# First layer and gates of a channel mix from softmax weights and packed values times the weight matrix, as a two-tap filter with three products for two tokens

## The chip, the cores and the metric

The kernel runs on one core of one Trainium2 chip. The metric is the time of one execution on the device in microseconds (us). The engines are named as the profile names them: PE is TensorE's matmul, PEld its weight load, DVE is VectorE, ACT is ScalarE, POOL is GpSimd, SP is SyncE, whose queue issues all DMAs here.

## The reference

```python
def sm_attn(qq, kk, vv):                       # softmax(scale * qq kk^T) vv
    ...
p_packed = sm_attn(p, k, v)                    # 32 packed rows for each head
out = sm_attn(q, p_packed, p_packed)           # 576 rows for each head
x = out.transpose(0, 2, 1, 3).reshape(B, S, H * D)
x_prev = np.concatenate([zeros, x[:, :-1, :]], axis=1)
xk = mu_k * x + (1.0 - mu_k) * x_prev
xr = mu_r * x + (1.0 - mu_r) * x_prev
k = np.maximum(xk @ w_k, 0.0)
v = k * k @ w_v
r = 1.0 / (1.0 + np.exp(-(xr @ w_r)))
return r * v
```

There are 8 sequences (B) of 576 tokens (S), 8 heads (H) of 64 columns (D), 32 packed rows for each head, 512 model columns and 1024 hidden columns. Weights come as 64-bit numbers and are turned into fp32 on the core. Everything is kept to fp32 accuracy: a product of two fp32 matrices is made of three products of a rounded part ("high", fp32r) and a rest ("low", fp32r): high by high, high by low, low by high.

## The kernel before, in words

The program is written as small generators, one for each piece of work. A planner (class Flow) holds a free time for each engine, costs such as `vec(n)` and `pe(us)`, pools of buffers with slots, and ranks; it takes the piece that could start first, ties by rank, and so fixes, at build time, the order of each engine's instructions. On the chip each engine then works through its list in that order.

For each sequence b, `front` makes the scores of the 32 packed rows of 8 heads (line 437, PE), `weights_of` their softmax, and the packed values `pm` (line 461, PE; 128 partitions are 4 head pairs by 32 rows, two heads side by side). They are transposed to `ppT` (line 482). `back` then does, for each half of the tokens, the scores of the tokens (line 541, PE), a softmax over 32 packed rows on transposed data (lines 553 to 576, mostly DVE, with one ACT exponential), and, at line 584 on PE, weights times packed values: that is x, with channels on partitions. `mixed_in` copies x from PSUM on ACT (line 606).

From there the work goes by 9 blocks of 512 tokens. `mix` makes xk and xr of a block on ACT and DVE (lines 639 and 643), `split` makes their high and low parts (lines 659 and 661). `gates` multiplies xr by w_r (lines 717 to 719, tile `pr`), `keys` multiplies w_k by xk (lines 678 to 680, tile `ph`), `values` multiplies the squared keys `sq` by w_v (lines 746 to 748, tile `pvo`). Each of these is a run of PE instructions of 512 columns. `squared` does relu, square, high part and low part (lines 689, 692, 696, 698); `gated` does the sigmoid (line 728); `done` multiplies (line 757) and writes 128 tokens by 512 columns to HBM with one DMA. `convert` loads a piece of a weight matrix and turns it into fp32 (lines 285 to 291) and into high and low parts (295, 297). In the first 50 us, while PE waits, the planner puts in matmuls without use (line 817, tile `spare`), so that PE's clock stays up.

PSUM has four slots `m` of one bank for the block matmuls and two slots `pa` of two banks for everything else.

Of the kernel before, what the change touches and what calls it, by code (L numbers as in the profile page):

```python
# [163 lines left out]
def attn_pack_channel_mix(ctx: ExitStack, tc: tile.TileContext, q, k, v, p, mu_k, mu_r, w_k, w_v, w_r, out):  # L164
# [5 lines left out]
    NG = H // 4  # L170
    NPR = H // 2
    HS = S // 2
    NTB = S // 32
    NQ = 4 * P
    NC = DM // P
    NF = DF // P
    TB = 512
    NB = B * S // TB
    NT = TB // P
    WP = 512  # L180
    scale = 1.0 / float(D) ** 0.5
    eps = 1e-9

    flow = Flow()


    FIRST = 10.09, 10.29
    RANK_1, RANK_MIX, RANK_W, RANK_V, LOADS_1 = 14.28, 11.5, 13.6, 15.2, 14.29
# [7 lines left out]
    def act(n, after=None, table=None):  # L196
        return "scalar", 0.14 + 0.72e-3 * n, after, table

    def pool(n, after=None):
        return "gpsimd", 0.1 + 2.2e-3 * n, after, None  # L200
# [14 lines left out]
    TR = dict(kT=0.0, qT=0.0)  # L215
    HALVES = slice(0, 64), slice(64, P)

    def reached():

        yield None, 0.0, None, None  # L220

    EARLY = 2
# [4 lines left out]
    BUFS = dict(raw=3, kq=4, vt=2, pt=1, a=2, aT=1, pm=2, e=2, a2=1, xt=4, tmp=4, xk=NC, sq=NF, sig=4,  # L227
                pa=2, both=1, m=4, staged=4)
# [9 lines left out]

    for tag in ("mx", "nmx", "rs", "sm", "free"):
        for j in range(2 if tag != "free" else 1):
            const.tile([P, 1 if "m" == tag[0] or "n" == tag[0] else 2], F32, name=f"{tag}{j}", tag=f"{tag}{j}")
    for tag, n, size in (
        ("xk", NC, 2 * TB), ("sq", NF, 2 * TB), ("tmp", 4, WP), ("sig", 4, DM), ("kq", 4, S), ("a", 2, S),
        ("raw", 3, S), ("a2", 1, S), ("e", 2, S), ("aT", 1, 5 * P), ("vt", 2, NPR * 4 * D),
    ):
        for j in range(n):
            sb.tile([P, size], F32, name=tag, tag=f"{tag}{j}")

# [5 lines left out]
    mus = const.tile([P, 4, NC], F32, name="mus")  # L256
# [3 lines left out]
    wk_h = const.tile([P, NC, DF], F32R, name="wk_h")  # L260
    wk_l = const.tile([P, NC, DF], F32R, name="wk_l")
    wr_h = const.tile([P, NC, DM], F32R, name="wr_h")
    wr_l = const.tile([P, NC, DM], F32R, name="wr_l")
    wv_h = const.tile([P, NF, DM], F32R, name="wv_h")
    wv_l = const.tile([P, NF, DM], F32R, name="wv_l")

    def convert(w, hi, lo, c, o, n, event, first=None):

        rank = flow.now.rank
        if first:  # L270
            flow.now.rank = first
        staged = yield from flow.take("staged")
        slot = yield from flow.take("sq")
        st = tile_([P, 2 * WP], U32, "sq", slot, "st")
        yield from load(st[:, :2 * n], w[c * P:(c + 1) * P, o:o + n].bitcast(U32), 0.46, 3.5e-3 * n)
        flow.now.rank = rank
        yield from reached()
        sm = yield from flow.take("tmp")
        m = tile_([P, WP], U32, "tmp", sm, "m")[:, :n]
        w0, w1 = (st[:, :2 * n].rearrange("p (n two) -> p two n", two=2)[:, j, :] for j in range(2))  # L280

# [8 lines left out]
        flow.give("sq", slot)  # L292
        flow.give("staged", staged)
        yield act(n)
        nc.scalar.copy(hi[:, c, o:o + n], m.bitcast(F32))
        yield vec(n)
        nc.vector.tensor_tensor(lo[:, c, o:o + n], m.bitcast(F32), hi[:, c, o:o + n].bitcast(F32), op=ALU.subtract)
        flow.give("tmp", sm)
        flow.set(event)

    ts, vts, pts, xts, xt2 = {}, {}, {}, {}, {}
# [8 lines left out]
    def loads(b):  # L310
        flow.spawn(packed(b), lrank(b) - (0.03 if b else 0.015))
        for src, tag in ((k, "kT"), (v, "vt"), (q, "qT")):
            if tag == "vt":
                for h in range(2):
                    flow.spawn(values_of(b, h), lrank(b) - 0.01)
                continue
# [529 lines left out]
```

## Time and profile before

| what | value |
|---|---|
| runs of before | 605.46, 605.8 (median), 606.75 us |
| profiled execution | span 605.1 us (first to last instruction) |
| mean granted TensorE clock | 0.997 |
| PE busy | 593.7 us, 98% of the span |
| DVE busy | 363.9 us, 60% |
| ACT busy | 331.0 us, 55% |
| DMA | 49.43 MB, mean 82 GB/s |

The profile's own execution is one whose span is 0.7 us below the median of the runs; the rest of the program's time lies around the span. In the rows of a timeline, the first number is the start in us from the start of the span, the second how long the row's group lasted, and "xN" how many instructions it holds. An fp32 matmul instruction appears as two records (the order of the program has 30 `spare` matmuls where the timeline has 60), an fp32r matmul and a transpose as one. A busy PE is not a PE at its peak: a matmul lasts longer than the step from its start to the start of the next.

### The profile page before, as it was taken

The numbers are of one execution on the slowest core, as the hardware profiler recorded it, in microseconds if no ns is written. First come the engines' busy times: TensorE is split into PE (matmuls) and PEld (weight loads), VectorE is DVE, ScalarE is ACT, GpSimd is POOL, SyncE is SP. The second block draws the span as 40 slices with busy tenths as digits, with TensorE's granted clock in tenths as the row PEclk, the third lists the DMA queues.
The fourth block names the chain that finished last, engine by engine and source line by source line (L and its number), as shares of the span: only waits on it lengthen the run. The fifth ranks groups of instructions, "written<-read, shape, count | busy, mean of one in ns | idle before, by whom it ended". The sixth has DMA issues, their size and how long they took to land.

```text
span 605.1 us, 10174 instructions
## 1 busy us (share of the span) xinstructions
PE 593.7 (98%) x3984; PEld 471.1 (78%) x3984; DVE 363.9 (60%) x701; ACT 331.0 (55%) x579; POOL 2.1 (0%) x23
## 2 busy tenths in 40 slices
PE   8899999999999999999999999999999999999997
PEld 7787777777777777777877787778788888888886
DVE  1499999949688479556765577166503822451321
ACT  4478784775774648454845485457534803641420
POOL 0000000000000000000000000000000000000000
PEclk9899999999999999999999999999999999999999
DMA  8895561764634646346034702000010010001001
GB/s 189 248 266 136 216 155 34 166 126 88 113 60 137 118 70 139 99 74 143 1 103 64 144 1 72 20 1 0 26 45 1 0 70 0 2 0 71 0 2 69
DMA packets 159184, 49.43 MB, mean 82 GB/s; under 512 B 143776, under 2 KB 151968, under 8 KB 159136
## 3 DMA queue, kind: packets, MB, share of 16 engines
q1 hardware_dynamic: 159136, 48.79, 34.0%
q8 instruction: 31, 0.51, 0.3%
q14 instruction: 17, 0.14, 0.1%
HBM read 39.33 MB, written 9.44 MB: 81 GB/s over the span
## 4 chain that ended last, share of the span: by engine, by line
PE 84%; DVE 5%; ACT 4%; SPq 3%; DMA 2%; issue 1%; ACTq 0%
PE pvo L746 11%; PE ph L678 10%; PE pvo L747 10%; PE pvo L748 10%; PE ph L680 10%; PE ph L679 10%; PE pr L717 5%; PE pr L719 5%; PE pr L718 5%; SPq L207 3%; PE pa L461 2%; PE pa L584 2%; DMA st<-in_moe_w_r 1%; PE pa L541 1%; ACT x L639 1%; DVE m L289 1%
## 5 line engine op out<-in xcount | busy, mean ns | idle before, releaser
L678 PE MATMUL ph<-xk,wk_h 128*128 128x512 f32 x288 | 114.8, 399 | 0.0
L746 PE MATMUL pvo<-wv_h,sq 128*128 128x512 f32 x288 | 113.9, 395 | 0.0
L679 PE MATMUL ph<-xk,wk_h 128*128 128x512 f32 x288 | 112.4, 390 | 0.0
L680 PE MATMUL ph<-xk,wk_l 128*128 128x512 f32 x288 | 112.3, 390 | 0.0
L747 PE MATMUL pvo<-wv_l,sq 128*128 128x512 f32 x288 | 112.3, 390 | 0.0
L748 PE MATMUL pvo<-wv_h,sq 128*128 128x512 f32 x288 | 112.2, 390 | 0.0
L689 ACT ACTIVATE r<-ph 128x512 f32<-128x512 f32 x72 | 43.0, 598 | 90.7 <-PE ph L680 89.7
L696 DVE CAST sq<-r 128x512 fp32r<-128x512 f32 x72 | 30.3, 420 | 100.6 <-ACT r L692 98.4
L746 PEld LDWEIGHTS pvo<-wv_h,sq 128*128 128x128 f32 x288 | 54.1, 188 | 15.9 <-issue 4.5
L678 PEld LDWEIGHTS ph<-xk,wk_h 128*128 128x128 f32 x288 | 54.1, 188 | 15.5 <-issue 4.5
L643 DVE SCALAR_TENSOR_TENSOR x<-xt,mus,x 128x512 f32<-128x512 f32 (+7 forms) x128 | 60.4, 513 | 6.0 <-ACT x L639 5.9
L680 PEld LDWEIGHTS ph<-xk,wk_l 128*128 128x128 f32 x288 | 54.1, 188 | 11.5
L748 PEld LDWEIGHTS pvo<-wv_h,sq 128*128 128x128 f32 x288 | 54.1, 188 | 11.4
L639 ACT ACTIVATE x<-xt,mus 128x512 f32<-128x512 f32 (+7 forms) x128 | 62.0, 530 | 1.5 <-DVE xr L661 1.3
L747 PEld LDWEIGHTS pvo<-wv_l,sq 128*128 128x128 f32 x288 | 54.1, 188 | 10.7
L679 PEld LDWEIGHTS ph<-xk,wk_h 128*128 128x128 f32 x288 | 54.2, 188 | 10.3
L717 PE MATMUL pr<-wr_h,xr 128*128 128x512 f32 x144 | 58.7, 408 | 0.0
L719 PE MATMUL pr<-wr_h,xr 128*128 128x512 f32 x144 | 56.7, 394 | 1.0 <-DVE xr L661 1.0
L718 PE MATMUL pr<-wr_l,xr 128*128 128x512 f32 x144 | 56.3, 391 | 0.0
L728 ACT ACTIVATE sig<-pr 128x512 f32<-128x512 f32 x36 | 21.3, 601 | 60.1 <-PE pr L719 56.5
L698 DVE TENSOR_TENSOR sq<-r,sq 128x512 fp32r<-128x512 f32 x72 | 49.4, 686 | 1.4
L757 DVE TENSOR_TENSOR sig<-pvo,sig 128x512 f32<-128x512 f32 x36 | 23.9, 686 | 38.8 <-PE pvo L748 38.8
(80 smaller groups left out, 727.5 us busy)
## 6 DMA issues: line engine op xcount, KB each, us to landing
out<-sig SPq DMA_DIRECT2D x36, 256.0 KB, 2.1
vt<-in_v SPq DMA_DIRECT2D x16, 512.0 KB, 4.6
raw<-in_k SPq DMA_DIRECT2D x96, 72.0 KB, 2.8
raw<-in_q SPq DMA_DIRECT2D x96, 72.0 KB, 2.8
st<-in_moe_w_k SPq DMA_DIRECT2D x8, 512.0 KB, 6.0
st<-in_moe_w_v SPq DMA_DIRECT2D x8, 512.0 KB, 5.5
raw<-in_k SPq DMA_DIRECT2D x16, 144.0 KB, 2.9
raw<-in_q SPq DMA_DIRECT2D x16, 144.0 KB, 5.1
```

The lines of the kernel that those rows point to most:

```text
L639: nc.scalar.mul(x32[:, o:o + n], xts[b, c][:, 1 + s:1 + s + n], mus[:, j, c:c + 1])
L643: nc.vector.scalar_tensor_tensor(x32[:, o:o + n], xts[b, c][:, s:s + n], mus[:, j + 1, c:c + 1], x32[:, o:o + n], op0=ALU.mult, op1=ALU.add,)
L678: nc.tensor.matmul(ph, wk_h[:, c, fs], xh, start=(c == 0), stop=False)
L679: nc.tensor.matmul(ph, wk_h[:, c, fs], xl, start=False, stop=False)
L680: nc.tensor.matmul(ph, wk_l[:, c, fs], xh, start=False, stop=(c == NC - 1))
L698: nc.vector.tensor_tensor(hl[:, 1, :], r, hl[:, 0, :].bitcast(F32), op=ALU.subtract)
L717: nc.tensor.matmul(pr, xh[:, ts_], wr_h[:, c, :], start=(c == 0), stop=False)
L718: nc.tensor.matmul(pr, xh[:, ts_], wr_l[:, c, :], start=False, stop=False)
L719: nc.tensor.matmul(pr, xl[:, ts_], wr_h[:, c, :], start=False, stop=(c == NC - 1))
L746: nc.tensor.matmul(pv[t], sh, wv_h[:, f, :], start=(f == 0), stop=False)
L747: nc.tensor.matmul(pv[t], sh, wv_l[:, f, :], start=False, stop=False)
L748: nc.tensor.matmul(pv[t], sl, wv_h[:, f, :], start=False, stop=(f == NF - 1))
```

## The change

The packed values times the weight matrix are made once for each sequence, and the tokens' softmax weights A multiply that directly; x, xk and xr are no longer made. With G = packed values times w, and Gm = (mu times packed values) times w, a token's row of xk times w_k is A[t] Gm + A[t-1] (G - Gm). For a pair of tokens, even e and odd o, and the odd token before it, that is

- y0 = A[e] G, shared by the pair,
- even token: y0 + (A[o before] - A[e]) (G - Gm),
- odd token: y0 + (A[o] - A[e]) Gm.

These are three products for two tokens, each over 256 rows (8 heads by 32 packed rows, two PE passes of 128) where before each token's product ran over 512 channels (four passes). Tokens are ordered by even and odd (288 each), and all outputs have channels on partitions, so that each sequence is one unit of 576 tokens.

New or changed: `taps` multiplies the packed values (plain, times mu_k, times mu_r: tile `pps`) by a chunk of 256 columns of w_k or w_r in fp32 (line 683, 16 instructions a chunk, 6 chunks a sequence), `taps_of` makes from it G, Gm and G - Gm with high and low parts (tile `G`, three buffers); `prep` makes the three moving operands `ehl` (one buffer) with high and low parts from `even` and `odd`; `main` runs the three products (line 748, tile `y`, 288 columns) and then `values` (line 815, tile `pvo`, 288 columns); `summed` drains y: ACT copies y0 to both places' common half, DVE adds the other two (line 775); then relu, two squares and the low part, or the sigmoid. `done` multiplies, transposes 32 by 32 on DVE and writes 32 partitions at a time, 128 bytes a piece, with four DMAs for each 128 channels. For the first sequence (`WHOLE = 1`) taps and products are plain fp32 without high and low parts. w_k and w_r are only turned into fp32; w_v still gets high and low parts. Buffers: raw 3 to 2, vt 2 to 1.

```diff
-        ppT = sb.tile([P, P], F32, name="ppT", tag="ppT")
+        pp = tile_([P, 3, P], F32, "pps", s3)
...
+        for j in range(2):
+            yield vec(P)
+            nc.vector.tensor_tensor(pp[:, 1 + j, :] ..., pp[:, 0, :] ..., mus[:, j, :] ..., op=ALU.mult)
...   # back(): up to the softmax over 32 rows as before, then
-        nc.vector.transpose(a2.rearrange("p (a b) -> p a b", b=32), e)
-        ...
-        px = [banks(slot) for slot in slots]
-        for pr in range(NPR):
-            own = slice(32 * pr, 32 * pr + 32)
-            for h, half in enumerate(HALVES):
-                nc.tensor.matmul(px[pr // 2][half, pr % 2, :HS], pm[own, h, :], a2[own, h * HS:(h + 1) * HS], ...)
+        if b:
+            yield from flow.wait(("apart", b - 1))
+        if hf:
+            nc.vector.transpose(odd.rearrange("p a (c b) -> p a c b", b=32)[:, :, 1:, :], blocks)
+            nc.scalar.copy(odd[:, :, 1:32], odd[:, :, HS:HS + 31])
+        else:
+            nc.vector.transpose(even.rearrange("p a (c b) -> p a c b", b=32), blocks)
...
-    def mixed_in(b, hf, g, slot, px): ...
-    def mix(i, j, res, tag): ...
-    def split(i, c, space, sx, x32, res, tag, slot): ...
-    def keys(i): ...
-    def gates(i): ...
+    def prep(b):                    # b >= WHOLE; the first sequence has one fp32 part and no split
+        yield from flow.wait(("A", b, 0), ("A", b, 1))
+        for shifted in (odd[:, :, :HS], odd[:, :, 32:]):
+            nc.vector.tensor_tensor(d, shifted, even, op=ALU.subtract)
+        yield from flow.wait(("used", b - 1))
+        for j, (st, x) in enumerate([(None, even)] + parts):
+            nc.scalar.copy(ehl[:, j, 0], x)
+            nc.vector.tensor_tensor(ehl[:, j, 1], x, ehl[:, j, 0].bitcast(F32), op=ALU.subtract)
+    CHUNKS = ("k", 0), ("k", 1), ("r", 0), ("r", 1), ("k", 2), ("k", 3)
+    def taps():
+        for b in range(B):
+            for n, (kind, cc) in enumerate(CHUNKS):
+                sg = yield from flow.take("G")
+                slot = yield from flow.take("pa")
+                for mat, j in ((0, 0), (1, 1 if kind == "k" else 2)):
+                    for pr in range(NPR):
+                        for h, own in enumerate(HALVES):
+                            nc.tensor.matmul(
+                                pg[32 * pr:32 * pr + 32, h, mat * GW:(mat + 1) * GW],
+                                pp[own, j, 32 * pr:32 * pr + 32], w[own, pr, o:o + GW], start=True, stop=True)
+    def taps_of(b, n, sg, slot, pg):        # b >= WHOLE
+        nc.scalar.copy(g[:, 0, :, 0:2, :], both)                                             # 1024
+        nc.scalar.copy(x, both[:, :, 1, :])                                                  # 512
+        nc.vector.tensor_tensor(g[:, 1, :, 0:2, :], both, g[:, 0, :, 0:2, :], op=ALU.subtract)  # 1024
+        nc.vector.tensor_tensor(x, both[:, :, 0, :], x, op=ALU.subtract)                     # 512
+        nc.scalar.copy(g[:, 0, :, 2, :], x)                                                  # 512
+        nc.vector.tensor_tensor(g[:, 1, :, 2, :], x, g[:, 0, :, 2, :], op=ALU.subtract)      # 512
+    def main():
+        for b in range(B):
+            for n, (kind, cc) in enumerate(CHUNKS):
+                for half in range(2):
+                    for j, mat in enumerate((0, 2, 1)):
+                        slot = yield from flow.take("m")
+                        terms = ((0, 0),) if b < WHOLE else ((0, 0), (0, 1), (1, 0))
+                        for h in range(2):
+                            for hl, el in terms:
+                                nc.tensor.matmul(y, g[:, hl, h, mat, cols], ehl[:, j, el, h, :], ...)
+            yield from values(b)
+    def summed(b, kind, f, j, slot, y):
+        if j == 0: nc.scalar.copy(s[:, 1, :], y)
+        else:      nc.vector.tensor_tensor(s[:, j - 1, :], y, s[:, 1, :], op=ALU.add)
+        ...        # after the last: sigmoid on ACT, or relu, square to high, square on ACT, low on DVE
...
-                nc.tensor.matmul(pv[t], sh, wv_h[:, f, :], ...)      # 128x512, three of them
+                        for w, x in ((0, 0), (0, 1), (1, 0)):
+                            nc.tensor.matmul(pv[par], wvs[f][:, w, cols], hl[:, x, par, :], ...)   # 128x288
-        yield from load(out[t0:t0 + P, :], sig, 0.63, 0.75)
+        nc.vector.transpose(oT.rearrange("p (u e) b -> p e u b", e=2), sig.rearrange("p e (u b) -> p e u b", b=32))
+        for i in range(4):
+            yield from load(rows[:, :, c:c + 32], oT[32 * i:32 * i + 32], 0.63, 0.41)
```

How the change moves instructions is shown at three places. PE in the steady part: first before, in the values of a block, where the scores of the next sequence's packed rows (line 437) stand between them.

```order
L746 MATMUL pvo<-wv_h,sq 128x512
L747 MATMUL pvo<-wv_l,sq 128x512
L748 MATMUL pvo<-wv_h,sq 128x512
L437 MATMUL pa<-kT,pt 32x288 x16
L746 MATMUL pvo<-wv_h,sq 128x512
L747 MATMUL pvo<-wv_l,sq 128x512
```

Now, the products of the third sequence, up to its values.

```order
L748 MATMUL y<-ehl,G 128x288 x30
L683 MATMUL pa<-wr,pps 32x256 x16
L748 MATMUL y<-ehl,G 128x288 x36
L683 MATMUL pa<-wk,pps 32x256 x16
L748 MATMUL y<-ehl,G 128x288 x36
L683 MATMUL pa<-wk,pps 32x256 x16
L748 MATMUL y<-ehl,G 128x288 x36
L683 MATMUL pa<-wk,pps 32x256 x16
L748 MATMUL y<-ehl,G 128x288 x36
L683 MATMUL pa<-wk,pps 32x256 x16
L748 MATMUL y<-ehl,G 128x288 x36
L815 MATMUL pvo<-sq,wv 128x288 x18
```

A run of taps now stands after nearly every chunk of 36 products, and the matmuls of line 584 are gone.

VectorE in the steady part, before: the softmax of a sequence's tokens between the squares of a block's keys.

```order
L696 CAST sq<-r 128x512
L698 TENSOR_TENSOR sq<-r,sq 128x512
L553 STREAM_TRANSPOSE e<-pa 128x576 x2
L560 TENSOR_REDUCE m_2654<-e 128x18
L560 TENSOR_REDUCE m_2661<-e 128x18
L562 TENSOR_TENSOR e<-e,m_2654 128x576
L696 CAST sq<-r 128x512
```

Now, in the products of the third sequence: the adds that empty PE's banks (line 775), the splits of the taps (712, 714, 719), the softmax weights of the next sequence (621, 649) and the squares (796).

```order
L775 TENSOR_TENSOR sig<-y,sig 128x288
L621 STREAM_TRANSPOSE odd<-e 128x2x288
L775 TENSOR_TENSOR sig<-y,sig 128x288
L775 TENSOR_TENSOR s<-y,s 128x288
L712 TENSOR_TENSOR G<-pa,G 128x2x512
L775 TENSOR_TENSOR s<-y,s 128x288
L649 TENSOR_TENSOR d<-odd,even 128x576
L775 TENSOR_TENSOR s<-y,s 128x288
L714 TENSOR_TENSOR g_3025<-pa,g_3025 128x512
L775 TENSOR_TENSOR s<-y,s 128x288
L719 TENSOR_TENSOR G<-g_2936,G 128x2x256
L796 TENSOR_TENSOR sq<-s,sq 128x576
```

Work that PE waits for (775) now alternates with work that is needed later.

VectorE where the first unit's values end and the second unit begins, before (757 is the last step of the first block, 661 makes the operands of the second).

```order
L661 TENSOR_TENSOR xr<-x_1333,xr 128x512
L661 TENSOR_TENSOR xk<-x_1334,xk 128x512
L643 SCALAR_TENSOR_TENSOR x_1380<-xt,mus,x_1380 128x64
L661 TENSOR_TENSOR xr<-x_1360,xr 128x512
L643 SCALAR_TENSOR_TENSOR x_1380<-xt,mus,x_1380 128x448
L643 SCALAR_TENSOR_TENSOR x_1397<-xt,mus,x_1397 128x64
L643 SCALAR_TENSOR_TENSOR x_1397<-xt,mus,x_1397 128x448
L364 STREAM_TRANSPOSE kT<-raw 128x576
L643 SCALAR_TENSOR_TENSOR x_1418<-xt,mus,x_1418 128x64
L643 SCALAR_TENSOR_TENSOR x_1418<-xt,mus,x_1418 128x448
L757 TENSOR_TENSOR sig<-pvo,sig 128x512 x2
```

And now (830 and 838 are the last steps of the first sequence, 649 and 659 make the operands of the second).

```order
L830 TENSOR_TENSOR sig<-pvo,sig 128x288
L838 STREAM_TRANSPOSE oT<-sig 128x2x9x32
L649 TENSOR_TENSOR d<-odd,even 128x576 x2
L387 STREAM_TRANSPOSE kT<-raw 128x576
L659 TENSOR_TENSOR ehl<-even,ehl 128x576
L659 TENSOR_TENSOR ehl<-d,ehl 128x576
L545 TENSOR_REDUCE mx<-pa 128x1
L659 TENSOR_TENSOR ehl<-d,ehl 128x576
```

The second unit's operands stood ahead of the first unit's last step; now they stand behind it. For the later sequences they stand ahead of the last of these steps.

## Prediction before the changed kernel was run

> **What bounds the kernel now.** I read the page first, then busy time by windows, then PE's timeline.
>
> ```profile
> PE 593.7 (98%) x3984; PEld 471.1 (78%) x3984; DVE 363.9 (60%) x701; ACT 331.0 (55%) x579; POOL 2.1 (0%) x23
> PE 84%; DVE 5%; ACT 4%; SPq 3%; DMA 2%; issue 1%; ACTq 0%
> 222.00:232.00 10.00, 10.00 (x57) 7.67 (x57) 10.00 (x23) 6.99 (x15) 0.00 (x0) 1.00 0.67 158
> 53.35:601.30 547.95, 546.27 (x3482) 429.84 (x3480) 331.05 (x640) 297.81 (x516) 1.22 (x12) 1.00 0.29 67
> ```
>
> The second row is the chain that ended last: 84% on PE. In the window rows the first number is the length, then PE, PEld, DVE, ACT. From 53.35 us on, PE is never idle for more than 1.7 us in all; the granted clock there is 1.00. In 222 to 232 us VectorE is also full (10.00 of 10) and PE still does not stop. So PE is the bound, and its price is the step from one start to the next.
>
> ```profile
> 299.71 0.39 PE L747 MATMUL pvo<-wv_l,sq 128*128 128x512 f32 x1
> ...
> 305.38 0.39 PE L748 MATMUL pvo<-wv_h,sq 128*128 128x512 f32 x1
> 305.70 1.20 PE L437 MATMUL pa<-kT,pt 64*32 64x288 f32 x32
> 306.83 0.50 PE L746 MATMUL pvo<-wv_h,sq 128*128 128x512 f32 x1
> 307.16 0.40 PE L747 MATMUL pvo<-wv_l,sq 128*128 128x512 f32 x1
> 307.40 0.39 PE L748 MATMUL pvo<-wv_h,sq 128*128 128x512 f32 x1
> 307.63 0.40 PE L746 MATMUL pvo<-wv_h,sq 128*128 128x512 f32 x1
> ```
>
> The first two rows are 25 steps apart: 226.7 ns for 512 columns, new weights each time. The sixteen small fp32 matmuls of line 437 cost 307.63 - 305.38 = 2.25 us less four ordinary steps (0.91), so 1.34 us. A sequence's share of block work is 240 x 9/8 = 270 steps, 61.2 us. The dense stretch holds 2139 of the 2160 block matmuls (484.9 us) and seven fronts: (547.9 - 484.9 - 1.7) / 7 = 8.8 us a front.
>
> **The price of a 288-column step** is not in the trace. Nearest rows:
>
> ```profile
> 13.07 0.64 PE L520 MATMUL pa<-ident,a 128*128 128x128 f32 x4
> L520 PE MATMUL pa<-ident,a x64: 270/284/387, 13.1 to 381.4; 128*128 128x128 f32 x64
> 23.70 1.20 PE L541 MATMUL pa<-qT,ppT 64*32 64x288 f32 x32
> 24.83 6.96 PE L817 MATMUL spare<-ident 128*128 128x128 f32 x60
> ```
>
> Fills (line 817) step by (6960 - 275) / 59 = 113 ns, a record and a 128-wide weight load each; transposes (line 520), with new weights each, by (640 - 284) / 3 = 119 ns. So a weight load does not hold a step above about 119 ns, although a load is listed with 188 ns. If the time per column alone counted, 512 columns at 2.4 per ns are 213.3 ns, and 226.7 is 13.4 ns more. The same surplus shows in the transposes (128 columns at two cycles are 106.7; 119 is 12 more). I take it as a fixed part of each step: 120 + 13.4 = 133.4 ns. The lower bound is that it goes with the columns: 226.7 x 288/512 = 127.5 ns. The upper bound is a step held by the weight load, 188 + 38 = 226.7 ns at any width; the fills exclude it.
>
> **The change, part by part.**
>
> PE, a sequence from the second on. Products: 216 steps, values: 192 steps; 408 x 133.4 = 54.4 us, against 61.2. The matmuls of line 584 go:
>
> ```profile
> 192.76 0.39 PE L719 MATMUL pr<-wr_h,xr 128*128 128x512 f32 x1
> 193.08 0.74 PE L584 MATMUL pa<-a,pm 32*64 32x288 f32 x16
> ...
> 194.55 0.40 PE L717 MATMUL pr<-wr_h,xr 128*128 128x512 f32 x1
> ```
>
> The last row starts four block steps after the first, with line 584 between them: 194.55 - 192.76 less four steps is 0.88 us, twice a sequence: the front falls from 8.8 to 7.0. New are six chunks of taps, each sixteen fp32 matmuls of the shape of line 437 with 256 columns. Of 1.34 us, four rounds of eight concurrent matmuls go with the columns (two cycles each, so 26.7 ns less a round): 1.34 - 0.11 = 1.23; six are 7.4 us. The lower bound is the streaming alone, 4 x 0.213 = 0.85. Sum for a sequence: 54.4 + 7.0 + 7.4 = 68.8 us, against 61.2 + 8.8 = 70.0. A quarter of the first layer's columns is saved, and most of it goes back to the fixed part of shorter steps and to the taps.
>
> VectorE, in the products of a sequence:
>
> ```profile
> 217.20 1.44 DVE L553 STREAM_TRANSPOSE e<-pa 128x576 f32<-128x576 f32 x2
> 218.56 1.37 DVE L560 TENSOR_REDUCE m<-e 128x18 f32<-128x576 f32 x2
> ...
> 221.52 0.68 DVE L698 TENSOR_TENSOR sq<-r,sq 128x512 fp32r<-128x512 f32 x1
> 222.12 0.75 DVE L566 TENSOR_REDUCE z<-e 128x18 f32<-128x576 f32 x1
> ```
>
> Steps of 0.68 us for 576 elements and 0.60 for 512: about 0.08 us and 1.04 ns an element. So 0.38 for 288 and 1.14 for 1024. In the fourth sequence's products, between the first and the last add, the order holds 24 adds (9.1 us), 7 lows of squares (4.8), 5 splits of 1024 and 9 of 512 (11.2), 13 other passes of 576 (8.8) and small ones (0.6): 34.5 us. PE needs there 216 x 133.4 ns and five taps, 35.0 us. The two are level, and PE can run ahead by four banks only, 3.2 us of products. Where VectorE was full before (222 to 232 us) PE lost nothing, so the lower bound of the wait is 0; the upper I set at 3.5 us, two splits of 1.14 and two passes of 0.6 standing ahead of an add. I take 1.0 us in each of six such stretches. In the values VectorE has 20 us of work in 33 and waits. ScalarE, at 0.47 to 0.5 us for 512 elements (rows below), has there 12 copies of 288 (3.6 us), 25 passes of 576 (14), the splits' 14 copies (9.2) and a table load (1.3), 28 of 35 us, and is not the bound.
>
> ```profile
> 209.05 0.59 ACT L526 COPY aT<-pa 128x512 f32<-128x512 f32 x1
> 209.52 0.62 ACT L689 ACTIVATE r<-ph 128x512 f32<-128x512 f32 x1
> ```
>
> **The start.** Before, PE's first gate is at 44.67 and the gates are dense from 53.35, as weights' high and low parts arrive:
>
> ```profile
> 23.52 0.43 DVE L287 TENSOR_SCALAR m<-m 128x512 uint32<-128x512 uint32 x1 [1.57 <-ACT m L285]
> 23.98 0.69 DVE L289 SCALAR_TENSOR_TENSOR m<-st,m 128x512 uint32<-128x512 uint32 x1
> 24.71 0.69 DVE L291 SCALAR_TENSOR_TENSOR m<-st,m 128x512 uint32<-128x512 uint32 x1
> 25.32 1.44 DVE L553 STREAM_TRANSPOSE e<-pa 128x576 f32<-128x576 f32 x2
> 44.67 0.48 PE L717 MATMUL pr<-wr_h,xr 128*128 128x512 f32 x1
> 53.35 0.40 PE L717 MATMUL pr<-wr_h,xr 128*128 128x512 f32 x1
> ```
>
> Now, from 25.3 us VectorE has twelve passes of 576 ahead of the first operands (8.2), three weight pieces of 1.8 us (23.52 to 25.32), mu's products and small ones (0.9): operands at 40, with two more passes 41.2. PE has 60 fills (13.6 us) after 24.83, two taps from 40 to 42.4 and six fills: first product at 44.0. The first sequence in fp32: an instruction is two records of 240 + 6 ns, 72 x 0.49 = 35.3 us; values 25.6; seven taps 8.6; the second sequence's front 7.0 and its 16 groups of raw transposes at 0.26 (six transposes and the step to the next fill are 0.52):
>
> ```profile
> 31.66 0.69 PE L387 MATMUL pa<-ident,raw 96*128 96x96 f32 x6
> 32.18 0.41 PE L817 MATMUL spare<-ident 128*128 128x128 f32 x2
> ```
>
> 4.2 us. PE alone would be through at 124.7. VectorE has from 41.2 us to the second sequence's operands 16 weight pieces (29 us), 8 lows of w_v (4.9), 24 adds and 8 lows of squares (14.5), the splits of seven taps (11), the second front and softmax (12), the first sequence's last steps (5.8) and transposes (5): 82 us, so 123: level again, 2 us for that. And as the order shows, these operands stand behind the first sequence's last step: product, transpose, two differences, a transpose and two lows, 4.2 us after the last matmul, of which line 437's 1.3 us is covered: 3 us. Second sequence's products at 130. The weights come in the same twenty loads, w_k now first. SP's queue gets 92 more issues (128 outputs instead of 36), by the 0.56 us of the rows at the end 52 us over the whole span, where SPq holds 3% of the chain: I cost them at nothing, with the loads a sequence ahead as cover. If that cover goes, the transposed k and q come late, then `even` and `odd`, and PE stops before a sequence's products.
>
> **From there.** 7 x 408 = 2856 steps 380.8, 39 taps 48.2, six fronts less one line 437 40.7: 599.7; six waits: 605.7.
>
> **The end.**
>
> ```profile
> 600.72 1.37 DVE L757 TENSOR_TENSOR sig<-pvo,sig 128x512 f32<-128x512 f32 x2
> 600.98 0.39 PE L748 MATMUL pvo<-wv_h,sq 128*128 128x512 f32 x1
> 600.76 1.69 SPq L207 DMA_DIRECT2D out<-sig  x3
> out<-sig SPq DMA_DIRECT2D x36, 256.0 KB, 2.1
> raw<-in_k SPq DMA_DIRECT2D x96, 72.0 KB, 2.8
> ```
>
> The last matmul starts at 600.98 and the span ends 4.1 us later. Now: drain 0.3, product 0.45, transpose 0.75, four issues instead of one (0.59 each), landing as the 128-byte pieces of the loads, 2.8 instead of 2.1: 7.0 us. DMA: Bandwidth & Descriptors of the Trainium skill (Specifications) says that pieces under 512 bytes make the DMA engine read, modify and write; no row here shows such a write, and an estimate of one more landing would put 2.8 us on the sum.
>
> Sum: 605.7 + 7.0 = 612.7, and 0.7 for what lies around the span (605.8 against 605.1): **613 us**, 1.2% slower.
>
> **Rivals.** A difference under 0.2% can't be told from none here.
>
> *The surplus goes with the columns* (127.5 ns). For it: one width alone is in the trace; against it: the transposes' 12 ns. The values save 1536 x 5.9 ns = 9.1 us; in the products PE falls to 33.7 us below VectorE's 34.5, so 0.5 in six and 1.3 in the last: 13 us less, 600. It is the case on the other side: it decides where the step is 129.7 ns or less. In the same direction, TensorE: Matmul & The Clock Gate of the Trainium skill (Back-to-back issue gap) gives a gap of N/2.4 + 2.5 ns; here 512 columns take 226.7 ns where that gives 215.8, so the trace does not agree; by it 288 columns are 122.5 ns and the time an estimated 591, to which I give 0.05 of this case's chance.
>
> *VectorE's work is hidden*: six waits and the 5 us at 125 to 130 vanish, as in 222 to 232 us: 602. Against it: that stretch was 10 us long, not 35.
>
> *VectorE becomes the bound of the products*: each add stands behind splits that wait for the taps and ScalarE, 3.5 us in each stretch: 628; at 5 us 637. For it: 34.5 of 35.0 us with no slack.
>
> **How the numbers follow.** Forecast 0.50 (605 to 619, with taps of 1.10 to 1.23 us and waits of 0.5 to 2.0); columns 0.20, all faster; hidden 0.13, nearly all faster; VectorE's bound 0.17. Faster 0.31, same 0.06, slower 0.63. The range leaves out a tenth at each end: 595 to 630.
>
> **What would show it.** Steps of lines 748 and 815: 133 ns (127 the first rival). Taps: 1.2 us. First product at 44, second sequence's at 130. PE's idle time ahead of line 748, put down to DVE's adds (775): about 1 us a sequence, 3.5 or more in the last rival. Last matmul to end of span 7 us. I would be wrong if the 288-column step is far from 133 ns, or if in-order waits between ScalarE and VectorE add up.

## The result, and the profile after

| kernel | median of the runs | lowest to highest | ratio to before |
|---|---|---|---|
| before | 606.12 us | 605.46 to 606.75 | 1 |
| changed | 614.45 us | 614.36 to 615.84 | 1.0143 (95% interval 1.0128 to 1.0157) |

The change costs 8.3 us, 1.4%. Ratios and intervals, here and below, leave out a run that is more than 1.5% above the fastest of its kernel, which is one run, in the experiment on the queue. The profiled execution took 614.51 us, its span is 612.7 us, the mean granted clock 0.990.

The page of the changed kernel, first the busy times, then the chain that ended last:

```profile
PE 591.3 (97%) x6264; PEld 524.2 (86%) x6264; DVE 456.8 (75%) x845; ACT 366.1 (60%) x639; POOL 0.8 (0%) x8
PE 69%; DVE 10%; DMA 6%; ACT 6%; SPq 4%; issue 3%; DVEq 0%; ACTq 0%
```

PE is still 97% busy, but its share of the chain has fallen from 84% to 69%: VectorE (93 us more busy than before), loads and ScalarE hold more of it.

Busy time by windows of the changed kernel (length, then PE, PEld, DVE, ACT, POOL; the first number behind them is the granted clock). The rows are: the first sequence from its first product to the second sequence's; the second sequence's products; three short pieces around their start; one steady stretch of products (the fourth sequence) and the values behind it.

```profile
42.57:131.07 88.50, 83.69 (x798) 64.29 (x796) 77.78 (x147) 58.48 (x102) 0.00 (x0) 0.99 0.48 119
131.07:177.50 46.43, 43.94 (x533) 36.80 (x531) 37.30 (x73) 35.22 (x62) 0.00 (x0) 0.95 0.36 63
129.00:132.50 3.50, 3.43 (x26) 2.02 (x26) 2.66 (x5) 0.00 (x0) 0.00 (x0) 0.53 0.86 187
132.50:136.00 3.50, 1.85 (x12) 1.21 (x11) 1.56 (x5) 3.25 (x7) 0.00 (x0) 0.99 0.70 109
136.00:139.50 3.50, 3.50 (x50) 2.98 (x49) 0.99 (x3) 0.87 (x3) 0.00 (x0) 0.51 0.70 109
278.79:313.69 34.90, 34.90 (x378) 31.40 (x377) 33.79 (x63) 30.29 (x53) 0.00 (x0) 1.00 0.33 60
313.69:347.39 33.70, 32.95 (x381) 29.87 (x380) 20.82 (x40) 13.28 (x23) 0.00 (x0) 1.00 0.47 82
```

In the steady products PE is busy all of 34.90 us beside a VectorE that is busy 33.79. In the second sequence the stretch is 11.5 us longer; part of that is a front that stands in the values elsewhere, part PE's waits and the pieces at half clock.

PE's timeline of the changed kernel, at three places: the end of the first sequence's values and the start of the second's products; two chunks of steady products with the taps between them; the last values.

```profile
124.45 0.70 PE L472 MATMUL pa<-kT,pt 64*32 64x288 f32 x12
129.07 2.07 PE L472 MATMUL pa<-kT,pt 64*32 64x288 f32 x20 [3.92 <-DVE kT L387]
131.07 1.74 PE L748 MATMUL y<-ehl,G 128*128 128x288 f32 x6
134.14 0.75 PE L563 MATMUL pa<-ident,a 128*128 128x128 f32 x4 [1.34 <-ACT a L556]
...
284.70 5.07 PE L748 MATMUL y<-ehl,G 128*128 128x288 f32 x36
289.70 1.09 PE L683 MATMUL pa<-wk,pps 64*32 64x256 f32 x32
290.73 5.07 PE L748 MATMUL y<-ehl,G 128*128 128x288 f32 x36
295.72 1.09 PE L683 MATMUL pa<-wk,pps 64*32 64x256 f32 x32
...
580.47 25.76 PE L815 MATMUL pvo<-sq,wv 128*128 128x288 f32 x192
```

The last matmul of that last row starts at 605.94: 191 steps in 25.47 us are 133.4 ns each. A chunk and its taps repeat every 6.02 us (295.72 - 289.70); 36 steps are 4.80, so the taps cost 1.22. In the first rows PE stands 3.92 us ahead of the third sequence's packed scores, which its list has in front of the second sequence's products. VectorE's rows for the second sequence's operands in that time are these:

```profile
125.68 0.78 DVE L838 STREAM_TRANSPOSE oT<-sig 128x576 f32<-128x576 f32 x1
126.38 1.38 DVE L649 TENSOR_TENSOR d<-odd,even 128x576 f32<-128x576 f32 x2
128.24 0.78 DVE L387 STREAM_TRANSPOSE kT<-raw 128x576 f32<-128x576 f32 x1 [0.48 <-issue]
128.94 0.72 DVE L659 TENSOR_TENSOR ehl<-even,ehl 128x576 fp32r<-128x576 f32 x1
```

The operands of the first product are whole when the last of these ends, at 129.66; the product starts 1.4 us later, behind the scores.

The end of the changed kernel, by the timeline:

```profile
605.87 0.86 DVE L830 TENSOR_TENSOR sig<-pvo,sig 128x288 f32<-128x288 f32 x2 [4.73 <-PE pvo L815]
606.76 0.78 DVE L838 STREAM_TRANSPOSE oT<-sig 128x576 f32<-128x576 f32 x1
607.57 2.60 SPq L210 DMA_DIRECT2D out<-oT  x4
```

The outputs' row among the DMA issues (KB each, median us to landing):

```profile
out<-oT SPq DMA_DIRECT2D x128, 72.0 KB, 2.2
```

Where the 7.6 us between the two spans lie can be counted from the first full step. Before, the dense block matmuls amount to a start at 48.6 (53.35 less 21 steps that stand ahead of it). The first product now starts at 42.57, 6.0 us earlier. The first sequence takes 88.5 us where a sequence took 70.0: 18.5 more. The seven others take 474.9 us (131.07 to 605.94) where they took 482.4 (600.98 - 48.6 - 70.0): 7.5 less. The end takes 6.8 instead of 4.1: 2.7 more. So the change does save time in the steady part, but less than the first sequence and the end cost.

### The profile page after: what moved, and what is told of

Same layout as the page of the kernel before. It is cut to its first block, busy times and chain, and to the rows that moved or that the text cites. A ratio compares the mean times of both kernels' runs of the same rounds, so it can differ in the third digit from the quotient of the medians.

```text
span 612.7 us, 15121 instructions
## 1 busy us (share of the span) xinstructions
PE 591.3 (97%) x6264; PEld 524.2 (86%) x6264; DVE 456.8 (75%) x845; ACT 366.1 (60%) x639; POOL 0.8 (0%) x8
## 4 chain that ended last, share of the span: by engine, by line
PE 69%; DVE 10%; DMA 6%; ACT 6%; SPq 4%; issue 3%; DVEq 0%; ACTq 0%
PE y L748 31%; PE pvo L815 25%; PE pa L683 7%; SPq L210 4%; DMA vt<-in_v 3%; PE pa L496 2%; DMA vl<-in_v 2%; PE pa L584 1%; ACT s L794 1%; ACT sq L792 1%; PE pa L472 1%; DMA raw<-in_q 1%; DVE s L775 1%; ACT G L708 1%; ACT s L788 1%
## 5 line engine op out<-in xcount | busy, mean ns | idle before, releaser
L748 PE MATMUL y<-ehl,G 128*128 128x288 f32 x1656 | 253.9, 309 | 1.4 <-ACT sig L767 0.6
L748 PEld LDWEIGHTS y<-ehl,G 128*128 128x128 f32 x1656 | 230.8, 189 | 26.0 <-issue 10.4
L815 PE MATMUL pvo<-sq,wv 128*128 128x288 f32 x1536 | 217.4, 298 | 0.0
L815 PEld LDWEIGHTS pvo<-sq,wv 128*128 128x128 f32 x1536 | 206.6, 188 | 10.1 <-issue 7.5
L775 DVE TENSOR_TENSOR s<-y,s 128x288 f32<-128x288 f32 x128 | 56.8, 449 | 10.2 <-PE y L748 7.2
L796 DVE TENSOR_TENSOR sq<-s,sq 128x576 fp32r<-128x576 f32 x64 | 47.9, 749 | 15.7 <-ACT s L794 15.6
L712 DVE TENSOR_TENSOR G<-pa,G 128x1024 fp32r<-128x1024 f32 x42 | 51.1, 1216 | 1.8 <-ACT g L710 1.8
L788 ACT ACTIVATE s<-s 128x576 f32<-128x576 f32 x64 | 43.7, 684 | 11.3 <-DVE s L775 10.5
L708 ACT CAST G<-pa 128x1024 fp32r<-128x1024 f32 x42 | 42.4, 1010 | 11.8 <-PE pa L683 11.3
L794 ACT ACTIVATE s<-s 128x576 f32<-128x576 f32 x64 | 43.9, 686 | 2.0
L792 ACT ACTIVATE sq<-s 128x576 fp32r<-128x576 f32 x64 | 44.0, 687 | 0.5
L775 DVE TENSOR_TENSOR sig<-y,sig 128x288 f32<-128x288 f32 x64 | 28.4, 448 | 2.0 <-ACT sig L767 1.6
```

What stands on the lines that cost most here:

```text
L708: nc.scalar.copy(g[:, 0, :, 0:2, :], both)
L712: nc.vector.tensor_tensor(g[:, 1, :, 0:2, :], both, g[:, 0, :, 0:2, :].bitcast(F32), op=ALU.subtract)
L748: nc.tensor.matmul(y, g[:, hl, h, mat, cols], ehl[:, j, el, h, :], start=(h == 0 and hl + el == 0), stop=(h == 1 and (hl, el) == terms[-1]),)
L775: nc.vector.tensor_tensor(s[:, j - 1, :], y, s[:, 1, :], op=ALU.add)
L788: nc.scalar.activation(flat, flat, AF.Relu)
L792: nc.scalar.activation(hl[:, 0], s, AF.Square)
```

## The experiments

The theory after the result: PE is the bound, the fixed part of each step and the taps eat what the columns save, and VectorE is level with PE, so that shortening either engine alone is worth little. The rivals: VectorE is the bound; the taps or the fixed part are not what costs; the loss is the hand-over to the second sequence. All ratios are to the kernel before on the same chip; against the changed kernel (1.0143) the difference of the ratios times 606 us is given.

### The width of a step

In the values the columns depend on the block of hidden columns.

```diff
+ n = (288, 288, 256, 224, 192, 160, 128, 288)[f]
- pv[par], wvs[f][:, w, cols], hl[:, x, par, :],
+ pv[par][:, :n], wvs[f][:, w, cols], hl[:, x, par, :n],
```

> In the values, the columns of a step depend on the block of hidden columns: 288, 288, 256, 224, 192, 160, 128, 288 in turn, 192 steps each; the columns left out are missing in the result. Theory (a step is columns at 2.4 per ns and 13.3 ns fixed, with the weight load below it): 120, 106.7 ... for 256 and 224 columns would be 120.0 and 106.7 ns; where a weight load holds the step, it stops falling at 113 to 119 ns, so 256 columns 120 ns and every smaller width 113 to 119 ns. Rival (the surplus goes with the columns at first, as 133.3 at 288 would not tell from a floor): 256 columns 118.5, 224 103.7, 192 88.9, 160 74.1, 128 59.2 ns without a floor. Whole time by the theory 192 x (13 + 4 x 17) ns = 15 us less.

A single run took 608.57 us, 1.0034 of before, 6.6 less than the changed kernel; the runs of one kernel here lie 1.5 to 6.7 us apart, so this 6.6 is rough. The median from start to start in the trace is 133 ns for 288 columns, 119 for 256, and 112, 112, 111 and 112 for 224, 192, 160 and 128. Two rows of PE's timeline in the last values:

```profile
579.76 1.04 PE L816 MATMUL pvo<-sq,wv 128*128 128x224 f32 x8
581.73 1.50 PE L816 MATMUL pvo<-sq,wv 128*128 128x128 f32 x10
```

The window of these values, 192 steps:

```profile
577.02:600.00 22.98, 22.98 (x193) 22.98 (x192) 6.89 (x13) 2.62 (x4) 0.00 (x0) 1.00 0.23 40
```

Between the two starts of the timeline lie 18 steps of 224, 192, 160 and 128 columns: 1.97 us, 109 ns each, whatever the width. The columns with 13.3 ns fixed and a floor of 112 ns give 192 x (3 x 133.3 + 120 + 4 x 112) / 8 = 23.2 us for the 192 steps of the window, which lasts 22.98; without a floor the same sum is 20.8. The 119 ns at 256 lies between the two forecasts for that width and tells nothing; what shows the surplus to be fixed is 226.7 ns at 512 beside 133.4 at 288, where a share of the columns would be 127.5. The floor is new: it holds a step of 128 by 128 weights up at 112 ns. The first layer's 288 columns are 21 ns above it.

The 6.6 us are less than PE saved (2.5 us in the last values, eight times): from the second to the seventh sequence the values fell by 0.3 to 1.9 us only, the most where no front stands in them. PE then waits 8.0 us in all for v (2.6 in the changed kernel). The cover in the values is thin too.

### Taps twice

The sixteen matmuls of each chunk's taps are issued twice (`for _ in range(2):` around them).

> The sixteen matmuls of each tap are issued twice; nothing else changes. Theory (the taps are on the path at about 1.2 us each, PE bound): 48 x 1.0 to 1.2 us more, at least 0.85 for the streaming alone: +41 to +58 us, 655 to 672. Rival (the taps lie in PE time that VectorE's work would leave idle anyway): +0 to 15 us, 614 to 630.

639.09 us, 1.0524 (1.0501 to 1.0547): 23 us more, between the two forecasts. PE's timeline and two windows of this kernel (first sequence's values; second sequence's products):

```profile
288.23 1.96 PE L684 MATMUL pa<-wr,pps 64*32 64x256 f32 x64
290.12 5.06 PE L749 MATMUL y<-ehl,G 128*128 128x288 f32 x36
295.11 1.96 PE L684 MATMUL pa<-wk,pps 64*32 64x256 f32 x64
```

```profile
103.73:134.99 31.26, 31.26 (x347) 29.21 (x340) 25.82 (x46) 13.68 (x24) 0.00 (x0) 1.00 0.58 105
134.99:176.86 41.87, 41.87 (x611) 35.99 (x610) 37.03 (x72) 30.72 (x54) 0.00 (x0) 1.00 0.40 73
```

A chunk with its taps takes 6.88 us instead of 6.02: the second sixteen cost 0.86, which is the streaming (four rounds of 213 ns). So of the 1.22 us of a group 0.36 us goes beyond the streaming; as the second sixteen do not pay it, I put it down to the change from wide to small matmuls and back. On PE the second sixteen are 41 us for 48 groups. From the third sequence's products to the end this kernel takes 419.8 us where the changed one takes 397.6: 22.2 for 33 groups that cost 28.4. PE's idle time in that stretch shrinks from 3.9 to 0.8 us, which is half of the difference; the other half was not traced. Ahead of that, of 13 us only 2 are seen: PE has in this kernel no idle time and no half clock in the windows above. The taps are on the path in the steady part; the second unit had room for them.

### VectorE: more, less, and less of both

Two more passes for each split of the taps (the last low made three times):

> The last low of each split of the taps is done three times instead of once (two more VectorE passes of 512 elements, 1.2 us, for each of 42 chunks; 7.3 us a sequence, 51 us in all). Theory (VectorE is hidden, but level: 33.8 of 34.9 us busy in a sequence's products): six chunks bring VectorE to 40 or 41 us in the products, so they grow to 37 to 41 us and the time rises by 15 to 40 us (630 to 655). Rival (VectorE has room, since its work moves into the values where it waits): products below 35.5 us and 0 to 5 us in all (614 to 620).

657.34 us, 1.0827 (1.0803 to 1.085): 41 us more for 51 us of work, a little above the forecast. The products of the sixth sequence:

```profile
444.29:487.86 43.57, 40.78 (x452) 33.51 (x450) 36.60 (x72) 30.79 (x52) 0.00 (x0) 0.96 0.31 55
```

43.57 us; the stretch also holds a front that stands in the values in the changed kernel. PE's waits for VectorE's lows (`G`), splits (`g`) and adds now add up to over 15 us, and the clock falls below 1. VectorE had almost no room.

The other way, without the low parts of the taps:

```diff
- nc.vector.tensor_tensor(g[:, 1, :, 0:2, :], both, ...)      # 1024
- nc.vector.tensor_tensor(g[:, 1, :, 2, :], x, ...)           # 512
- y, g[:, hl, h, mat, cols], ehl[:, j, el, h, :],
+ y, g[:, 0, h, mat, cols], ehl[:, j, el, h, :],
```

> The low parts of the taps are not made (two VectorE passes of 1024 and 512 elements for each of 42 chunks), and the products read the high part in their place, so that PE has the same instructions; the product that uses the lows is left out of the result. VectorE has 42 x (1.14 + 0.60) = 73 us less. Theory (PE is the bound, VectorE is hidden in the steady products): a sequence's products stay at 34.9 us in the trace; only the hand-over from the first to the second sequence gains, since three chunks' lows (5 us) no longer stand ahead of the second sequence's operands: its products start at 126 to 128 instead of 131.1, and the half clock behind that gap may go: 605 to 610 us. Rival (VectorE is the bound of the products, or level with a wait in each): 7 us less a sequence in six or seven of them: 595 or less, with products of 33 us or less.

607.87 us, 1.001 (0.9991 to 1.003): 8 us less for 73 us of VectorE's work taken away. The fourth sequence's products last 35.55 us:

```profile
274.75:310.30 35.55, 35.16 (x378) 31.42 (x377) 24.50 (x50) 28.80 (x51) 0.00 (x0) 1.00 0.33 60
```

VectorE is busy 24.50 us instead of 33.79 and the stretch is no shorter: PE is the bound there. But the gain did not come from where I expected it: the second sequence's products start at 130.79, as before, and the half clock stays (0.92 from 131 to 176 us). The second sequence's products are 3.3 us shorter (its values 1.9 longer), and from the third sequence on the values with a front in them are 0.6 to 1.3 us shorter each.

Less on PE, with five of six steps of the products at 256 columns:

```diff
+ nc_ = HS if b < WHOLE or h + hl + el == 0 else 256
+ y[:, :nc_], g[:, hl, h, mat, cols], ehl[:, j, el, h, :nc_],
```

> From the second sequence on, five of the six steps of each product group take 256 columns instead of 288 (the missing 32 are left out of the result): 1260 steps x 14.3 ns = 18 us less on PE, nothing else changed. Theory (VectorE is level with PE in the products, 33.8 us busy of 34.9): PE's 2.6 us less in a stretch bring it under VectorE, so a stretch falls to 33.5 to 34.2 us, and the whole gains 4 to 9 us: 605 to 611. Rival (PE alone bounds the products): 34.9 falls to 32.3 us, the whole to 595 to 598.

609.39 us, 1.0046 (1.0021 to 1.0071): 6 us less for 18 us of PE. The fourth sequence's products:

```profile
280.30:313.59 33.29, 32.53 (x378) 28.70 (x377) 32.68 (x62) 29.25 (x51) 0.00 (x0) 1.00 0.33 60
```

1.6 of 2.6 us came through; now PE and VectorE are both below the length of the stretch, and PE waits in it twice (0.34 and 0.42 us, both put down to VectorE's splits of the taps, lines 714 and 719). Both edits together:

> The 256 columns in five of six steps and, with them, no low parts of the taps (left out of the result as in the run that did this alone). Theory (PE and VectorE level, each hiding the other): the two together gain more than their sum: VectorE has 7 us less in a sequence, so that PE's 18 us come through whole on top of the 6.5 of the run without lows: 589 to 592 us. Rival (VectorE never bounds the products): the sum of the two runs' gains to within 2 us, whatever these are.

593.73 us, 0.9782 (0.9757 to 0.9807): 22 us less, where the two alone gave 8 and 6.

```profile
270.65:303.62 32.97, 32.14 (x379) 28.59 (x377) 24.10 (x50) 28.22 (x50) 0.00 (x0) 1.00 0.35 65
```

The stretch falls by the whole 2.6 us against the one without lows (35.55). From the third sequence's products to the last matmul the changed kernel takes 397.6 us, without lows 393.0, with 256 columns 393.1, with both 381.4: 4.6, 4.5 and 16.2 us. The gains are not a sum. In the fourth sequence's products the two alone give -0.65 and 1.61 us and both together 1.93, and PE's waits for VectorE there are gone (0.8 us for ScalarE is left): each engine hides the other's gain. That is not shown for all of the 16.2 us, since the planner also orders the work anew: the third sequence's products (38.17 us with 256 columns, 32.86 with both) hold a group of line 584 in the first case alone, and the 4.4 us for which PE waits for v with 256 columns do not occur with both.

### The hand-over to the second sequence

Lows of w_v and of the first sequence's squares on GpSimd:

> The low parts of w_v (8 passes of 512) and of the first sequence's squares (8 passes of 576) go from VectorE to GpSimd: 10 us less on VectorE in the first unit, nothing else. Theory (the second sequence's products start at 131.1 instead of 124.7 because VectorE is behind there, and the two stretches at half clock that follow the idle 4 us cost 3.4 us): products at 125 to 127, no half clock, 605 to 609 us. Rival (the wait there is for loads that stand behind the output's issues, or GpSimd's lows come too late for PE): 612 us or more, and the gap at 125 to 131 stays or moves ahead of the first sequence's values.

613.99 us, 1.0119 (1.01 to 1.0139): 1.5 us less, with intervals that overlap. My theory fell. The second sequence's products did start earlier, at 128.46 (their first low ends at 124.07 instead of 129.66, and PE has no idle time ahead of them), but PE then stood at 130.2 for the third sequence's exponentials, and the clock fell as before: 46.66 us to its values. The first sequence's products lasted 58.6 us instead of 47.7, with work of the values moved into them and a wait of 2.4 us for a split; its values 29.1 instead of 40.8. Twenty matmuls without use between the values and the scores that PE waited for:

> Twenty fp32 matmuls without use (4.5 us) stand on PE behind the first sequence's values, ahead of the third sequence's packed scores, where PE stood idle for 3.9 us; the order of the work is otherwise the same. Theory (the idle time let the granted clock fall to half for two stretches of 3.4 us at 129 to 139 us): clock 1.00 there, the second sequence's products from start to values 43 to 44.5 us instead of 46.4, the whole 611 to 612.5 us. Rival (the half clock lies beside waits for VectorE and ScalarE and costs nothing): 614 to 615 us with the clock at 1.00.

614.93 us, 1.0141 (1.0117 to 1.0164): nothing. (The profiled run is the lowest of the six, 612.47 us.) The products started at 129.02, 2 us earlier, but the wait had moved behind their first steps:

```profile
130.00:132.50 2.50, 0.48 (x4) 0.40 (x4) 2.09 (x5) 1.79 (x3) 0.00 (x0) 1.00 0.52 82
133.50:137.50 4.00, 4.00 (x54) 3.34 (x53) 1.57 (x3) 1.33 (x4) 0.00 (x0) 0.57 0.70 109
```

PE is busy 0.48 of 2.50 us, and from 133.5 on the clock is at 0.57. Then with the third sequence's scores held behind the second's first product:

```diff
+ if b == 2:
+     yield from flow.wait("begun")       # in front, ahead of its scores
+ if (tag, b, pr) == ("kT", 2, NPR - 1):
+     yield from flow.wait("begun")       # in transposed, ahead of the last k
```

> As the fills alone, and the third sequence's packed scores with the last transpose of its k (VectorE) are held until the second sequence's first product has been issued. Theory (PE's in-order list has the third sequence's scores ahead of the second sequence's products, and these wait for VectorE's chain, not for VectorE's total work): the second sequence's products start at 128 to 129.5 us instead of 131.1, no half clock, the whole 608 to 611 us. Rival (VectorE is behind there whatever stands first): products at 130.5 to 132 us and 612 us or more.

611.39 us, 1.0078 (1.0058 to 1.0098): 4 us less, a little above the forecast. The second sequence's products, and its values:

```profile
130.07:170.49 40.42, 37.69 (x438) 33.63 (x437) 27.92 (x54) 30.30 (x55) 0.00 (x0) 1.00 0.43 80
170.49:205.20 34.71, 34.38 (x405) 29.99 (x402) 31.78 (x56) 16.28 (x26) 0.00 (x0) 1.00 0.43 77
```

The fills (tile `cover`) ahead of the products, and the last operand of the first product:

```profile
125.69 4.63 PE L768 MATMUL cover<-ident 128*128 128x128 f32 x40
129.01 0.75 DVE L663 TENSOR_TENSOR ehl<-even,ehl 128x576 fp32r<-128x576 f32 x1
```

No half clock, and a stretch 6.0 us shorter; but the front that left it makes the values 3.9 us longer (30.81 in the changed kernel, from 177.50 to 208.31). The products start 1.0 us earlier than in the changed kernel, later than I forecast: their operands are whole at 129.76, as late as in the changed kernel (129.66), so the hold took away the scores' share of the delay and not the operands'. At the end of these values the kernel is 3.1 us ahead (205.20 against 208.31); by the times it is 3.9. That much the hand-over is worth here, not the whole loss.

The first sequence made like the others (`WHOLE = 0`), the place where 18.5 us went:

> The first sequence is made like the others, from high and low parts (216 steps of 133.4 ns in place of 72 fp32 products of 0.49 us: 6.5 us less on PE; 6 more splits of the taps and 3 more lows of the operands on VectorE: 16 us more). Theory (in the first unit, from the first product to the second sequence's, VectorE is as full as PE, because it also converts the weights there): the unit does not get shorter than its 88.5 us, and the whole is 612 to 626 us. Rival (PE's fp32 products set the first unit's length): 82 to 84 us for the unit and 607 to 609 us for the whole.

631.72 us, 1.0382 (1.0336 to 1.0427): 15 us more, worse than either forecast. Windows of this kernel in its first unit:

```profile
60.00:80.00 20.00, 16.43 (x148) 13.05 (x148) 18.94 (x36) 16.60 (x28) 0.00 (x0) 0.91 0.56 170
80.00:100.00 20.00, 15.97 (x144) 13.57 (x142) 19.77 (x37) 14.46 (x26) 0.00 (x0) 0.83 0.00 1
```

VectorE is full (18.94 and 19.77 of 20 us), PE is not, and the clock falls. The first product starts at 51.17 (8.6 us later), the unit takes 96.4 us. VectorE, which converts the weights there, has no room for the splits as well; one wait of 3.3 us in the unit is put down to ScalarE's sigmoid. The fp32 products are the cheaper way.

### The queue of the loads

v's loads on GpSimd's queue from the third sequence on:

> From the third sequence on, the loads of v are issued on GpSimd's queue instead of SP's; all else keeps its queue. Theory (PE's waits for v in the values, 2.6 us in all and about as much around them, come from v's loads standing on SP's queue behind loads of q that wait for a buffer and behind the outputs' four issues): those waits vanish, 609.5 to 612.5 us. Rival (the loads are late because v's one buffer comes free late): the waits stay and the time is 614 to 616 us.

Three runs lie between 616.9 and 622.6 us, a fourth at 631.4. Without the fourth the ratio is 1.0203 (1.0165 to 1.0242): 3.6 us more; neither forecast. In the changed kernel PE waits for v as in the first rows of its waits (us in all, times, longest):

```profile
PE pa L472 <- DVE kT L387: 3.9, 1, 3.9
PE pa L496 <- DMA vt<-in_v: 2.6, 4, 1.1
```

That wait for v is gone in the profile of this kernel. But the planner set the front elsewhere: products of the fourth sequence 39.27 us instead of 34.90, values 29.97 (313.51 to 343.48) instead of 33.70, 0.6 more together. The profiled run is the lowest of the four; why they differ so, and what makes the median worse, was not settled.

### What the experiments point to

The fills, the hold, and besides the last low of each split on GpSimd (42 passes of 1.33 us there, 0.60 less on VectorE) and two of the last four output issues on ScalarE's queue:

> As the run with fills and the held third front; besides, the last low of each split of the taps goes to GpSimd (42 x 0.60 us less on VectorE), the hold comes after the transposes' buffer is taken, and of the last four outputs two are issued on ScalarE's queue. Theory: 611.4 us less 1.1 us at the end (two issues fewer in a row) and 2 to 3 us for a third of the lows' effect: 606 to 609 us. Rival (GpSimd's passes of 1.3 us or more come too late for the products, or hold VectorE up): 612 us or more.

608.89 us, 1.0041 (1.0022 to 1.006): 6 us less than the changed kernel, and still 0.4% slower than before. The granted clock is 0.999. Fills and hold together had given 4 us; what GpSimd's lows and the two issues add was not measured apart. No version here that makes the whole result beats the kernel before: the one at 0.9782 leaves out columns and the low parts of the taps.

## Why the prediction was right, point by point

The forecast was 613 us, in a range of 595 to 630; 614.45 were measured. The sum without what lies around the span was 612.7 us, and the span is 612.7. That the two agree so well is luck: against the forecast the first product came 1.4 us early, the first unit was 2.5 us longer (88.5 for 86), the stretch from there 0.8 and the end 0.2 shorter. The prices on which the direction rests, a step and a group of taps, were right.

- *The step of 288 columns*: forecast 133.4 ns, measured 133.4. The fixed surplus held; the rival by columns (127.5 ns) fell. The rule of TensorE: Matmul & The Clock Gate of the Trainium skill (Back-to-back issue gap), N/2.4 + 2.5 ns, gives 122.5 ns; the trace does not agree with it for these fp32r steps at either width (133.4 ns at 288 columns, 226.7 at 512).
- *The taps*: forecast 1.23 us, measured 1.22; on the path in the steady part, as doubling them showed.
- *The start*: first product forecast 44.0, measured 42.57; second sequence's 130, measured 131.07. The sum was near, and one of its reasons held: the operands stand behind the first sequence's last step. I took 4.2 us for that; the first of them are whole at 129.66, 5.2 us after PE is through with the values (124.45). Two terms failed. For VectorE being level I took 2 us, but it stood 0.57 us waiting for PE's last values at 124.16, so its earlier work was done, and taking lows off it brought 1.5 us at most. And I let line 437's scores (now line 472) fill 1.3 us of the wait. They stand there in PE's list, but most of them wait for the last transposed k: 0.70 us of them ran in the wait, and the others from 129.07 to 131.07, in front of the products and at half clock. Fills and hold, which take both away, gave 4 us.
- *The queue*: I costed SP's 92 more issues at nothing with the loads a sequence ahead as cover. The two last loads of k were issued from 124.96 on, behind four output issues, and VectorE's transpose waited 0.48 us for the second (2.5 to 2.7 us from issue to landing); PE's waits for v are 2.6 us in all. Small, but not nothing, and a queue of their own for v's loads did not give it back.
- *The waits in the products*: forecast 1.0 us in each of six stretches. PE stood still for 0 to 0.64 us in each stretch from the third sequence on, 1.0 in all six: the term was too large. Its 6 us came back elsewhere: half clock for two pieces of 3.4 us around the start of the second sequence (an estimated 3 us lost, not foreseen), its waits (1.34 and less), and waits in the values. From 131.07 to the last matmul it is 474.9 us against 475.7: errors that cancelled.
- *VectorE hidden* was a rival with 602 us. It is hidden in the steady products, as that rival said; its time failed because the hand-over's 5 us did not vanish. *VectorE the bound* (628 us) fell, but its ground, 34.5 of 35.0 us without slack (33.79 of 34.90 measured), was right: 51 us more of its work cost 41.
- *The end*: forecast 7.0 us (its parts as listed add up to 6.7), measured 6.8. The outputs landed in 2.2 us, not 2.8. DMA: Bandwidth & Descriptors of the Trainium skill (Specifications) says that pieces under 512 bytes are read, modified and written. Here 72 KB in such pieces landed in 2.2 us beside 2.1 for 256 KB in whole rows before; as the sizes differ, that neither shows nor excludes a price of it.
- *Around the span*: I took 0.7 us from the median of the runs and the span of one other execution; the changed kernel's profiled execution took 1.8 us more than its own span, and so did a run of before (606.87 us with a span of 605.1). This term was mis-sized by 1.1 us, most of the 1.5 by which the forecast of 613 was low.

## What to carry to other kernels

A change that trades columns for more and shorter steps has to be priced by the step, with its fixed part and its floor, and the small matmuls it adds with the switch to them and back. When two engines are level, shortening one bought little here and shortening both more than the sum: test a bound by loading and unloading each, and both. At a hand-over read the in-order list of the engine that waits first; the engine that is late is not always the one whose work should be cut.

## What the runs showed of the hardware that I had not expected

- A step with new 128 by 128 fp32r weights takes 111 to 112 ns (median) at 128 to 224 columns, 119 at 256, 133.4 at 288 and 226.7 at 512.
- The granted clock fell to half after short idle times of PE, but not after each. In the changed kernel it was 0.5 for 3.4 us from 129.2 on, behind 3.92 us of idle time, and again from 136.0 on, behind waits of 1.34 and 0.32 us; with the fills one gap of 2.02 us at 130.1 led to half clock from 133.9 on. A gap of 2.35 us at 136.4 in the kernel with fills and hold, and one of 2.36 us at 340.0 in the kernel with the widths, led to none. A fall lasted 3.4 us, twice that (lows on GpSimd; no lows of the taps) or three times that (v's loads on GpSimd's queue), and began 2.2 to 4.8 us behind the start of the idle time in these runs. The length of one gap alone does not decide; what does was not settled.
- One group of sixteen small fp32 matmuls costs 1.22 us when it stands between wide ones, 0.36 us beyond its streaming; a second group that follows at once costs 0.86 us, the streaming alone.
